# One fused layer with a local attention and a gated MLP: reordered QKV calls, another queue for three writes, and 22 identity transposes at the start

## The chip, the cores and the metric

The kernel runs on one core of one Trainium2 chip. The metric is the device time of one execution in microseconds (us). Its matrix engine is TensorE (PE in the profile, its weight loads PEld), beside VectorE (DVE), ScalarE (ACT), GpSimd (POOL) and SyncE (SP), which here only issues DMAs.

## The reference

The input x is 2048 tokens of D = 576, all in fp32. There are 32 heads of 18 columns, and the attention is local and dilated: token s looks at the 8 tokens s, s-2, ..., s-14.

```python
x = A_x
h = x + _A_ref(_layernorm(x, axis=-1), A_wqkv, A_wo)      # qkv, softmax over 8 places, times wo
h2 = h + _B_ref(_layernorm(h, axis=-1), B_w_gate, B_w_up, B_w_down)
...
g = jnp.einsum("bsd,df->bsf", x, w_gate)                  # F = 4608
u = jnp.einsum("bsd,df->bsf", x, w_up)
h = _sigmoid(g) * u
return jnp.einsum("bsf,fd->bsd", h, w_down)
```

## The kernel before

**Blocks and groups.** Even and odd tokens are apart (e = 0, 1), and each of these halves is cut in two: `BLOCKS` numbers the four blocks b = 0 to 3 of 512 tokens, (0,0), (0,1), (1,0), (1,1). A block is 4 token tiles of 128. The QKV weights are cut into four groups g of 8 heads, 432 columns each (q, k and v). A QKV *call* (b,g) is `qkv(b, g, T, w)`, lines 392 to 411: for each token tile 14 matmul passes (`tok_major`, lines 152 to 160; the fp32 operands are split into a high part `th` and a low part `tl`, so that a product takes the passes high-high, low-high and high-low), ScalarE copies the sum to `ev` (L403), and after the fourth tile the q, k and v of the call are written to DRAM scratch by three DMAs (L407, L409).

**Attention** is done by VectorE from that scratch (lines 166 to 230): SP loads q, a window of k and one of v (L176 to L178), and VectorE multiplies, reduces and normalises (L189 to L226). A generator `ag` gives it out in steps that the code takes between the QKV tiles. Its order is fixed in `att_all`: (0,0), (0,1), (1,0), (0,2), (0,3), (1,1), (1,2), (1,3), and then, under the MLP, blocks 2 and 3. The attention of (b,g) is only given out when the call (b,g) has been written (`emitted`). After (0,3) block 0 is complete, and L428 copies the tail of its rows.

**The opening** (lines 469 to 565) normalises the first tokens by chained instructions: statistics (L484 to L487, the power on POOL), `tok` (L491), transposes by the identity matrix on PE (L497, L499), the split of the transposes into `th` by ScalarE (`x_hi`, L504 and L505) and `tl` by VectorE (`x_lo`, L509 and L511), and of the first weights into high and low parts `qw` (L516, L519) from `wr`. The weights of group 1 come behind: three loads `ws` by SP (L386), split at L104 (ScalarE) and L105 (VectorE).

**The front** (L655 on) is the output projection of block 0: transposes of the attention's rows in two steps per token tile (`tr_main` L146, `tr_rest` L150), splits (L104, L105, L108, L109), the passes with `wo` and `wow`, the residual (L262), the second LayerNorm (L123 to L128) and its transposes. It is a generator `fr`, and its steps stand between the tiles of the calls (2,3) and (3,3). At its end ScalarE issues `hacc` (`h<-h`, L625) and the transposed rows (`x<-tok`, L627) to DRAM.

**The MLP** runs in units c = 0, 1, ...; its first matmuls are L746 and L753 with the weights `wf` (units 0 and 1) and `w` (unit 2 on, loaded by SP at L702 as `wg`, split at L104 and L105). The sigmoid is ScalarE's L793, the product VectorE's L766, the way down L864. Under it go, as background steps (`bg_step`, of which `skip` leaves some out), the rest of the attention and the projection of blocks 1 to 3, whose rows come back from DRAM as `oj` (L707).

**What orders the work.** The code's order, with priorities (`tc.high_priority`) and explicit "issue after" edges, goes to a scheduler, which gives each engine one list that is worked off in order; a waiting instruction holds all behind it. Releases of buffers and DMA landings are awaited in the lists.

Of the kernel before, what the change touches and what calls it, by code (L numbers as in the profile page):

```python
# [21 lines left out]
P = 128  # L22
# [9 lines left out]
TB = P * NS  # L32
# [28 lines left out]
def kernel(ctx, tc, x, wqkv, wo, wmlp, out):  # L61
    nc = tc.nc
    dve, act, pool, pe, sp = nc.vector, nc.scalar, nc.gpsimd, nc.tensor, nc.sync
# [14 lines left out]
    ident = cst.tile([P, P], F32, name="ident")  # L78
# [12 lines left out]
    qscr = [[dr.tile([P, NS * CG], F32, name=f"q{b}_{g}") for g in range(NG)] for b in range(4)]  # L91
# [61 lines left out]
    def tok_major(ps, n, th, tl, js, wh, wl):  # L153
        k = 0
        for c in range(4):
            for a, m in ((th, wh), (tl, wh), (th, wl)):
                pe.matmul(ps[:, :n], a[:, c, js], m[:, c], start=k == 0, stop=False)  # L157
                k += 1
        pe.matmul(ps[:, :n], th[:, 4, js], wh[:, 4], start=False, stop=False)
        return pe.matmul(ps[:, :n], th[:, 4, js], wl[:, 4], start=False, stop=True)  # L160
# [71 lines left out]
    def step(gen, n):  # L232
        for _ in range(n):
            if next(gen, END) is END:
                return
# [58 lines left out]
    def th_tile():  # L294
        return xt.tile([P, 5, TB], F32R, tag="th", bufs=3, name="th")

    def tl_tile():
        return xt.tile([P, 4, TB], F32R, tag="tl", bufs=4, name="tl")
# [24 lines left out]
    def mm_tile():  # L323
        return psp.tile([P, 512], F32, tag="mm", bufs=3, name="mm")

    def acc_tile():
        return psp.tile([P, 512], F32, tag="acc", bufs=5, name="acc")
# [7 lines left out]
    def ev_tile(shape):  # L335
        return sar.tile(shape, F32, tag="ev", bufs=2, name="ev")
# [59 lines left out]
    def qkv(b, g, T, w):  # L396
        e, hf = BLOCKS[b]
        ev = ev_tile([P, 3, NS, CG])
        for j in range(NS):
            ps = acc_tile()  # L400
            passes.append(tok_major(ps, NQ, *T, slice(j * P, (j + 1) * P), w[:, 0], w[:, 1]))
            with tc.high_priority(HI):
                act.activation(ev[:, :, j], ps[:, :NQ].rearrange("p (t c) -> p t c", t=3), AF.Copy)  # L403
            yield
        r0 = LP + hf * TB
        with tc.high_priority(HI):
            act.dma_start(qscr[b][g], ev[:, 0].rearrange("p j c -> p (j c)"))  # L407
            for t, s in ((1, kscr), (2, vscr)):
                act.dma_start(s[e][g][r0:r0 + TB, :].rearrange("(p j) c -> p (j c)", p=P),  # L409
                              ev[:, t].rearrange("p j c -> p (j c)"))  # L410
        emitted.add((b, g))

# [27 lines left out]
    ag = att_all()  # L440
    T = []
# [11 lines left out]
    def heads(order, ws, n):  # L453
        for b, g in order:
            for _ in qkv(b, g, T[b], ws[g]):
                step(ag, n)

    def opening():
        xb = load_x(0, (0, 1))
        wr = raw_w(0)  # L460
        load_x(0, (2, 3), xb)
        th, tl = th_tile(), tl_tile()
        xn = tok_tile()
        qw = saw.tile([P, 2, 5, NQ], F32R, tag="qw", bufs=2, name="qw")
        T.append((th, tl))
        w.append(qw)
        last = {}

        def ch(key, fn):
            with ExitStack() as way:  # L470
                way.enter_context(tc.high_priority(3 * HI))
                if key in last:
                    way.enter_context(tc.issue_after(getattr(last[key], "ins", last[key])))
                last[key] = fn()

        nr, pv, pr = {}, {}, {}

        def stats(j):
            bs = sm.tile([P, 2, 6], F32, bufs=4, name="bs")
            mv = sm.tile([P, 2], F32, bufs=4, name="mv")  # L480
            rstd = sm.tile([P, 1], F32, bufs=4, name="rstd")
            nr[j] = mv[:, 0:1], rstd
            for k in range(2):
                ch(dve, lambda: dve.bn_stats(bs[:, k], xb[:, j, k * DH2:(k + 1) * DH2]))  # L484
            ch(dve, lambda: dve.bn_aggr(mv, bs))
            ch(dve, lambda: dve.tensor_scalar(rstd, mv[:, 1:2], EPS, None, ALU.add))
            ch(pool, lambda: pool.tensor_tensor(rstd, rstd, mhalf, ALU.pow))  # L487

        def norm(j):
            m, r = nr[j]  # L490
            ch(dve, lambda: dve.tensor_scalar(xn[:, j, :D], xb[:, j], m, r, ALU.subtract, ALU.mult))  # L491
            ch(dve, lambda: dve.tensor_copy(xn[:, j, D:DX], xn[:, j, DM:D]))

        def tr(j):
            pv[j], pr[j] = mm_tile(), acc_tile()
            for c in range(4):
                ch(pe, lambda: pe.transpose(pv[j][:, c * P:(c + 1) * P],  # L497
                                            xn[:, j, c * P:(c + 1) * P], ident))
            ch(pe, lambda: pe.transpose(pr[j][:, :P], xn[:, j, DM:DX], ident))  # L499

        def x_hi(j):
            js = slice(j * P, (j + 1) * P)
            pv[j] = pv[j].rearrange("p (c n) -> p c n", c=4)
            ch(act, lambda: act.activation(th[:, 0:4, js], pv[j], AF.Copy))  # L504
            ch(act, lambda: act.activation(th[:, 4, js], pr[j][:, :P], AF.Copy))  # L505

        def x_lo(j):
            js = slice(j * P, (j + 1) * P)
            ch(dve, lambda: dve.tensor_tensor(tl[:, :, js], pv[j], f32(th[:, 0:4, js]),  # L509
                                              ALU.subtract))  # L510
            ch(dve, lambda: dve.tensor_tensor(th[64:128, 4, js], pr[j][64:128, :P],  # L511
                                              f32(th[64:128, 4, js]), ALU.subtract))
            ends.append(last[dve])

        def w_hi(c):
            ch(act, lambda: act.activation(qw[:, 0, c], wr[:, c], AF.Copy))  # L516

        def w_lo(c):
            ch(dve, lambda: dve.tensor_tensor(qw[:, 1, c], wr[:, c], f32(qw[:, 0, c]),  # L519
                                              ALU.subtract))  # L520

        call = qkv(0, 0, T[0], qw)
        ends = []

        def heads_of(j):
            ch(pe, lambda: (next(call), passes[-1])[1])

        stats(0)
        stats(1)
        norm(0)  # L530
        w_hi(0)
        tr(0)
        norm(1)
        w_hi(1)
        tr(1)
        w_lo(0)
        w_hi(2)
        w_lo(1)
        x_hi(0)
        x_lo(0)  # L540
        w_hi(3)
        w_lo(2)
        w_hi(4)
        stats(2)
        x_hi(1)
        w_lo(3)
        w_lo(4)
        heads_of(0)
        with tc.high_priority(3 * HI):
            n3, r3, sq = ln_stats(xb[:, 3], xn[:, 3])  # L550
        norm(2)
        tr(2)
        x_lo(1)
        heads_of(1)
        x_hi(2)
        ch(act, lambda: act.activation(xn[:, 3, :D], xb[:, 3], AF.Identity, bias=n3, scale=r3))
        ch(act, lambda: act.activation(xn[:, 3, D:DX], xn[:, 3, DM:D], AF.Copy))
        x_lo(2)
        tr(3)
        heads_of(2)  # L560
        x_hi(3)
        x_lo(3)
        heads_of(3)
        drain(call)
        return ends

    w = []
# [15 lines left out]
    w.append(qkv_w(2, wr))  # L583
    wr = raw_w(3)
    pads(2)
    heads(((2, 1), (3, 1)), w, 2)
    w.append(qkv_w(3, wr))
    pads(3)
    h = load_x(0)
    wos = [None, wo_w(1, swo.tile([P, 2, 5, DH2], F32R, tag="wo", name="wo1"))]  # L590
    heads(((0, 2), (0, 3), (1, 2), (2, 2), (3, 2)), w, 2)
    wos[0] = wo_w(0, saw.tile([P, 2, 5, DH2], F32R, tag="qw", bufs=2, name="wow"))

    banks = [0]
# [46 lines left out]
    fr = front()  # L641
# [10 lines left out]
        step(ag, 1)  # L652
    last = passes[-1]
    with tc.issue_after(getattr(last, "ins", last)):
        for _ in range(2):  # L655
            next(fr)
    for b in (2, 3):
        for j, _ in enumerate(more if b == 2 else qkv(b, 3, T[b], w[3])):
            with ExitStack() as way:
                if (b, j) == (2, 0):  # L660
                    way.enter_context(tc.issue_after(getattr(passes[-1], "ins", passes[-1])))
                next(fr, END)
            step(ag, 1)
        if b == 2:
            with tc.high_priority(2 * HI):
                wg = xt.tile([P, WC], F32, tag="tl", bufs=4, name="wg0")
                sp.dma_start(wg, wmlp[0])
                ww = first_split(wg)
# [377 lines left out]
    c = 0  # L1046
# [201 lines left out]
    for c, (kind, p, f) in enumerate(items):  # L1248
        w, d = wc
        for b, late_c in ((0, NF + NSTD - 3), (1, NF + NSTD + 5)):  # L1250
            if c == late_c:
                e, hf = BLOCKS[b]
                paced(ov[e, hf], hacc[b])
        skip = ((2, 3) if c == 0 else ()) if kind == "std" else (3,)
        by_seven = c >= NF + NSTD
        if c == NSTD:
            finish_bg()
# [110 lines left out]
```

## Time and profile before

| | us |
|---|---|
| three runs: median (lowest to highest) | 1578.9 (1578.4 to 1580.97) |
| the profiled execution, its own time | 1584.01 |
| its span on the core | 1582.2 |
| outside the span (1584.01 - 1582.2) | 1.8 |
| PE busy | 1551.0 (98%) |
| DVE busy | 1255.2 (79%) |
| ACT busy | 879.2 (56%) |
| POOL busy | 199.9 (13%) |

Every row of the timeline reads: start in us, length in us, engine, line, operation, output<-inputs, shape, xcount, and in brackets the time that the engine was idle before it and whose work it waited for. An engine with a q behind its name (SPq, ACTq) is issuing a DMA. A row with x4 or x5 is a run of such instructions.

### The profile page before, as it was taken

How to read it: one execution, taken by the hardware profiler on the slowest of the kernel's cores; microseconds unless marked ns; L12 is line 12 of the kernel's file. 1: busy time of each engine (PE TensorE's matmuls, PEld its weight loads, DVE VectorE, ACT ScalarE, POOL GpSimd, SP SyncE). 2: the span in 40 equal slices, each digit the busy share in tenths (PEclk: the TensorE clock that was granted, in tenths of full speed). 3: DMA queues.
4: the chain of work that ended last, by engine and by line, in shares of the span. 5: the costliest groups of instructions: out<-in, count | busy, mean ns of one | idle time of the engine just before them, and what ended most of it. 6: DMA issues, size and time to landing. Idle time of an engine off the chain costs nothing.

```text
span 1582.2 us, 22347 instructions
## 1 busy us (share of the span) xinstructions
PE 1551.0 (98%) x8520; PEld 1377.3 (87%) x8520; DVE 1255.2 (79%) x1883; ACT 879.2 (56%) x1584; POOL 199.9 (13%) x249
## 2 busy tenths in 40 slices
PE   8999999999999999999999999999999999999998
PEld 7999888887888888888888888888888888888887
DVE  6998999969999999999426588866777776677755
ACT  6632244435555645566542355766777766777660
POOL 2300000020000010000101010112112112111210
PEclk9999999999999999999999999999999999999999
DMA  8646445365566677664683524999899989999983
GB/s 284 215 168 220 179 185 190 108 235 183 133 167 170 164 176 192 157 162 109 161 242 125 181 81 126 193 181 177 170 180 186 173 173 181 173 173 186 181 169 120
DMA packets 77147, 273.95 MB, mean 173 GB/s; under 512 B 8336, under 2 KB 14224, under 8 KB 76144
## 3 DMA queue, kind: packets, MB, share of 16 engines
q0 software_dynamic: 28192, 107.29, 37.5%
q1 hardware_dynamic: 41216, 145.11, 27.2%
q10 hardware_dynamic: 7632, 20.12, 3.3%
q8 instruction: 66, 1.08, 0.3%
q14 instruction: 41, 0.34, 0.1%
HBM read 143.98 MB, written 130.87 MB: 174 GB/s over the span
## 4 chain that ended last, share of the span: by engine, by line
PE 58%; issue 16%; DVE 11%; DMA 8%; POOL 4%; ACT 2%; SPq 0%; ACTq 0%; POOLq 0%; DVEq 0%
PE b L746 27%; PE dp L864 13%; PE dp L926 6%; PE b L753 5%; PE acc L157 4%; POOL h L935 3%; DMA wg<-in_wmlp_dram 3%; DVE pr L189 2%; DVE pr L215 1%; DVE lg L193 1%; DVE w L105 1%; DVE pr L221 1%; PE b L157 1%; PE bgp L157 1%; DMA x<-tok 1%
## 5 line engine op out<-in xcount | busy, mean ns | idle before, releaser
L746 PE MATMUL b<-tl,w 128*128 128x512 f32 x1704 | 432.6, 393 | 5.1 <-ACT s L820 3.2
L746 PEld LDWEIGHTS b<-tl,w 128*128 128x128 f32 x1704 | 307.9, 188 | 63.6 <-ACT s L820 4.7
L746 PE MATMUL b<-th,w 128*128 128x512 f32 x1344 | 346.2, 392 | 1.5 <-DVE s L839 1.5
L746 PEld LDWEIGHTS b<-th,w 128*128 128x128 f32 x1344 | 244.8, 188 | 46.5 <-DVE s L839 1.9
L932 ACT ACTIVATE ev<-dp 128x576 f32<-128x576 f32 x224 | 144.7, 646 | 63.2 <-PE dp L926 58.9
L753 PE MATMUL b<-th,w 128*128 128x512 f32 x568 | 175.7, 390 | 0.0
L104 ACT ACTIVATE w<-wg 128x384 fp32r<-128x384 f32 (+1 forms) x186 | 110.8, 601 | 111.1 <-PE b L753 48.8
L935 POOL DMA_DIRECT2D h<-ev x128 | 110.0, 860 | 458.6 <-ACT ev L932 444.7
L157 PE MATMUL acc<-qw,th 128*128 128x432 f32 x512 | 154.3, 362 | 2.5 <-DVE th L109 2.3
L105 DVE TENSOR_TENSOR w<-wg,w 128x640 fp32r<-128x640 f32 (+1 forms) x186 | 120.8, 656 | 41.3 <-ACT w L104 41.1
L105 DVE TENSOR_TENSOR w<-tw,w 128x512 fp32r<-128x512 f32 x120 | 82.6, 688 | 82.1 <-ACT w L104 81.5
L753 PEld LDWEIGHTS b<-th,w 128*128 128x128 f32 x568 | 106.5, 188 | 23.2
L864 PE MATMUL dp<-d,h1h 128*128 128x288 f32 x640 | 119.9, 297 | 0.0
L864 PE MATMUL dp<-d,h0h 128*128 128x288 f32 x608 | 114.1, 297 | 0.8 <-DVE tail L874 0.8
L872 ACT ACTIVATE stage<-dp 128x576 f32<-128x576 f32 x104 | 66.9, 645 | 70.1 <-PE dp L864 69.8
L157 PEld LDWEIGHTS acc<-qw,th 128*128 128x128 f32 x512 | 96.6, 189 | 8.4 <-DVE th L109 3.5
L864 PEld LDWEIGHTS dp<-d,h1h 128*128 128x128 f32 x640 | 99.7, 190 | 3.0
L104 ACT ACTIVATE w<-tw 128x512 fp32r<-128x512 f32 x120 | 75.4, 628 | 46.5 <-PE b L746 40.0
L864 PEld LDWEIGHTS dp<-d,h0h 128*128 128x128 f32 x608 | 95.1, 190 | 4.3 <-DVE tail L874 1.0
L157 PE MATMUL acc<-qw,tl 128*128 128x432 f32 x256 | 92.6, 362 | 0.1
L189 DVE TENSOR_TENSOR pr<-kw,q 128x2304 f32<-128x2304 f32 x32 | 81.8, 2556 | 8.8 <-DMA kw<-k 8.7
L880 POOL DMA_DIRECT2D h<-stage x26 | 31.0, 1194 | 436.3 <-ACT stage L872 350.1
(310 smaller groups left out, 2955.5 us busy)
## 6 DMA issues: line engine op xcount, KB each, us to landing
h<-ev POOLq DMA_DIRECT2D x96, 576.0 KB, 7.1
wg<-in_wmlp_dram SPq DMA_DIRECT2D x47, 928.0 KB, 5.9
h<-stage POOLq DMA_DIRECT2D x26, 1152.0 KB, 9.5
wg<-in_wmlp_dram SPq DMA_DIRECT2D x36, 640.0 KB, 4.3
kw<-k SPq DMA_DIRECT2D x16, 792.0 KB, 5.2
vw<-v SPq DMA_DIRECT2D x16, 792.0 KB, 4.3
wd<-in_wmlp_dram SPq DMA_DIRECT2D x18, 576.0 KB, 7.4
h<-ev POOLq DMA_DIRECT2D x32, 288.0 KB, 6.9
```

What stands on the lines that cost most here:

```text
L104: act.activation(hi, src, AF.Copy)
L105: splits.append(dve.tensor_tensor(lo, src, f32(hi), ALU.subtract))
L157: pe.matmul(ps[:, :n], a[:, c, js], m[:, c], start=k == 0, stop=False)
L189: dve.tensor_tensor(pr, both(kw, u), q[:, us].unsqueeze(2).broadcast_to([P, 2, W, CG]), ALU.mult)
L746: pe.matmul(ps, wt[:, a, k0 + c], xx[:, m + c], start=first and k == 0, stop=k == 5, skip_group_check=True)
L753: pe.matmul(ps, wt[:, a, k0], xx[:, 4], start=False, stop=a == 1, skip_group_check=True)
L864: pe.matmul(ps[:, i, :DH2], a[:, js], d[:, m, i * DH2:(i + 1) * DH2], start=k == 0, stop=k == n)
L872: act.activation(hv, ps, AF.Copy)
L880: pool.dma_start(hacc[b], hs, accum_op=ALU.add, max_dma_last_dim=8 * D)
L926: pe.matmul(ps[:, i, :DH2], a[x][:, js], m[y], start=k in (0, 1, 3) and q == 0, stop=q == 2, skip_group_check=True)
L932: act.activation(hs[:, k % 2], ps[:, :, :DH2], AF.Copy)
L935: pool.dma_start(hsev[:, u, k0:k + 1], hs[:, :k + 1 - k0], accum_op=ALU.add, max_dma_last_dim=8 * D)
```

## The change

- The order of the QKV calls after (3,0): before (2,1), (3,1), (0,2), (0,3), (1,2), (2,2), (3,2); now (2,1), **(0,2)**, **(3,1)**, three tiles of (1,2), (0,3), the last tile of (1,2), (2,2), (3,2). The split of group 3's weights (`qkv_w(3, wr)`) still stands behind (3,1).
- The three writes of call (3,3) are issued by SP, not by ScalarE.
- In the front, one step (`tr_main` of token tile 0) is taken behind the second tile of (2,3), and the second step comes behind the next QKV tile; before, both came together.
- The MLP's unit c = 0 leaves out one background step less.
- Before all other PE work, 22 transposes of the identity into a PSUM tile that nobody reads.

```diff
         r0 = LP + hf * TB
         with tc.high_priority(HI):
-            act.dma_start(qscr[b][g], ev[:, 0].rearrange("p j c -> p (j c)"))
+            q = sp if (b, g) == (3, 3) else act
+            q.dma_start(qscr[b][g], ev[:, 0].rearrange("p j c -> p (j c)"))
             for t, s in ((1, kscr), (2, vscr)):
-                act.dma_start(s[e][g][r0:r0 + TB, :].rearrange("(p j) c -> p (j c)", p=P),
+                q.dma_start(s[e][g][r0:r0 + TB, :].rearrange("(p j) c -> p (j c)", p=P),
                               ev[:, t].rearrange("p j c -> p (j c)"))
...
         nr, pv, pr = {}, {}, {}
+        pre = mm_tile()
+        for _ in range(22):
+            ch(pe, lambda: pe.transpose(pre[:, :P], ident, ident))
...
-    heads(((2, 1), (3, 1)), w, 2)
+    heads(((2, 1), (0, 2), (3, 1)), w, 2)
     w.append(qkv_w(3, wr))
     pads(3)
     h = load_x(0)
     wos = [None, wo_w(1, swo.tile([P, 2, 5, DH2], F32R, tag="wo", name="wo1"))]
-    heads(((0, 2), (0, 3), (1, 2), (2, 2), (3, 2)), w, 2)
+    first = qkv(1, 2, T[1], w[2])
+    for _ in range(3):
+        next(first)
+        step(ag, 2)
+    heads(((0, 3),), w, 2)
+    for _ in first:
+        step(ag, 2)
+    heads(((2, 2), (3, 2)), w, 2)
...
     with tc.issue_after(getattr(last, "ins", last)):
-        for _ in range(2):
-            next(fr)
+        next(fr)
     for b in (2, 3):
         for j, _ in enumerate(more if b == 2 else qkv(b, 3, T[b], w[3])):
             with ExitStack() as way:
                 if (b, j) == (2, 0):
                     way.enter_context(tc.issue_after(getattr(passes[-1], "ins", passes[-1])))
+                    next(fr)
                 next(fr, END)
...
-        skip = ((2, 3) if c == 0 else ()) if kind == "std" else (3,)
+        skip = ((3,) if c == 0 else ()) if kind == "std" else (3,)
```

**ScalarE's list at the opening**, before:

```order
L516 ACT_TABLE_LOAD
L516 ACTIVATE qw<-wr 128x432 x3
L504 ACTIVATE th<-mm 128x4x128
L505 ACTIVATE th<-acc 128x128
L516 ACTIVATE qw<-wr 128x432 x2
L504 ACTIVATE th<-mm 128x4x128
L505 ACTIVATE th<-acc 128x128
L104 ACTIVATE qw<-ws 128x432 x2
```

and now (the lines of the changed file, so L520 is L516, L508 is L504 and L509 is L505):

```order
L520 ACT_TABLE_LOAD
L520 ACTIVATE qw<-wr 128x432 x3
L104 ACTIVATE qw<-ws 128x432 x3
L508 ACTIVATE th<-mm 128x4x128
L509 ACTIVATE th<-acc 128x128
L520 ACTIVATE qw<-wr 128x432 x2
L508 ACTIVATE th<-mm 128x4x128
L509 ACTIVATE th<-acc 128x128
```

All three splits of group 1's weights (`qw<-ws`) have moved ahead of the first `th`.

**VectorE's list at the front**, from the last attention instruction of (0,3) (`tok<-kw`) to the first splits of the projection's transposes (`tl<-mm`), before:

```order
L226 TENSOR_TENSOR tok<-kw 128x4x144
L189 TENSOR_TENSOR pr<-kw,q 128x2304
L428 COPY tok<-tok 128x64 x4
L193 TENSOR_REDUCE lg<-pr 128x128
L105 TENSOR_TENSOR tl<-mm,th 128x4x128
L109 TENSOR_TENSOR th<-acc,th 64x128 x3
```

and now:

```order
L226 TENSOR_TENSOR tok<-kw 128x4x144
L189 TENSOR_TENSOR pr<-kw,q 128x2304
L105 TENSOR_TENSOR wow<-ws,wow 128x288
L429 COPY tok<-tok 128x64 x4
L193 TENSOR_REDUCE lg<-pr 128x128
L189 TENSOR_TENSOR pr<-kw,q 128x2304
L193 TENSOR_REDUCE lg<-pr 128x128
L201 TENSOR_REDUCE mx<-lg 128x32
L105 TENSOR_TENSOR tl<-mm,th 128x4x128 x2
```

The second product and its reduction (L189, L193) and the maximum (L201) of the next attention now stand ahead of the first split.

**SP's list ahead of the MLP's first weight loads** (`wg` at the end; `vw` is the v window of an attention, `wg_2024` and `wg_2046` the weights of unit 0, `q_3_106`, `k_3_82`, `v_3_90` scratch in DRAM), before:

```order
L667 DMA wg_2024<-in_wmlp_dram 128x1856
L176 DMA q<-q_2_97 128x576
L178 DMA vw<-v_2_85 128x1584
L702 DMA wg<-in_wmlp_dram 128x1856 x3
```

and now:

```order
L678 DMA wg_2046<-in_wmlp_dram 128x1856
L178 DMA vw<-v_2_85 128x1584
L408 DMA q_3_106<-ev 128x576
L410 DMA k_3_82<-ev 128x576
L410 DMA v_3_90<-ev 128x576
L713 DMA wg<-in_wmlp_dram 128x1856 x3
```

The three writes of call (3,3) (`<-ev`) have come in ahead of the weight loads, and the q load went ahead of `wg_2046`.

## Prediction

> **What bounds the kernel now.** I read the page first, then PE's waits, then the windows, and the timeline only at the places of the change.
>
> ```profile
> span 1582.2 us, 22347 instructions
> PE 1551.0 (98%) x8520; PEld 1377.3 (87%) x8520; DVE 1255.2 (79%) x1883; ACT 879.2 (56%) x1584; POOL 199.9 (13%) x249
> ```
>
> PE is the bound: 1582.2 - 1551.0 = 31.2 us of idle time is all that any reordering can win. PE's waits say where it lies:
>
> ```profile
> PE mm L497 <- DVE tok L491: 6.6, 1, 6.6
> PE b L146 <- DMA oj<-o: 4.2, 1, 4.2
> PE acc L157 <- DVE th L109: 2.3, 2, 1.6
> PE mm L150 <- DVE tok L428: 1.7, 1, 1.7
> PE mm L150 <- DVE tok L128: 0.4, 1, 0.4
> ```
>
> The 6.6 us are the kernel's start (first loads and statistics). The change touches the start, the front (L428, L109 and L128: 1.7 + 1.6 + 0.4) and, further off, the read-back `oj`. The windows (length, PE's busy time and count, then PEld, DVE, ACT, POOL, the granted clock, DMA share, GB/s) say what the QKV stage between them is like:
>
> ```profile
> 60.00:80.00 20.00, 19.34 (x105) 17.92 (x104) 19.48 (x18) 7.76 (x19) 4.08 (x3) 1.00 0.70 237
> ...
> 120.00:140.00 20.00, 20.00 (x104) 19.15 (x103) 14.91 (x11) 3.72 (x7) 0.94 (x1) 1.00 0.72 256
> ...
> 300.00:320.00 20.00, 15.77 (x82) 13.50 (x81) 13.52 (x20) 6.75 (x12) 1.45 (x2) 0.94 0.39 136
> 320.00:340.00 20.00, 20.00 (x127) 18.57 (x126) 12.52 (x27) 6.27 (x13) 0.56 (x1) 0.89 0.67 254
> ```
>
> From 60 to 80 PE idles 0.66 us, from 120 to 140 not at all, though VectorE idles 5.1 there. Two windows at the read-back show what an idle PE costs beside the wait: a clock of 0.94 and 0.89.
>
> **The opening: +3.7 us.** The 22 transposes themselves lie in PE's first 6.6 idle us. But ScalarE's list has changed with them: the three splits of group 1 (`qw<-ws`) stand ahead of the first `th`. Before:
>
> ```profile
> 4.98 1.41 SPq L386 DMA_DIRECT2D ws<-in_wqkv_dram  x3
> 6.59 1.12 PE L497 MATMUL mm<-ident,tok 128*128 128x128 f32 x4 [6.59 <-DVE tok L491]
> 7.75 0.60 ACT L504 ACTIVATE th<-mm 128x512 fp32r<-128x512 f32 x1 [0.50 <-PE mm L497]
> 8.74 0.69 DVE L509 TENSOR_TENSOR tl<-mm,th 128x512 fp32r<-128x512 f32 x1
> 9.94 1.15 ACT L104 ACTIVATE qw<-ws 128x432 fp32r<-128x432 f32 x2
> 13.17 0.66 PE L497 MATMUL mm<-ident,tok 128*128 128x128 f32 x4
> 13.38 0.69 DVE L509 TENSOR_TENSOR tl<-mm,th 128x512 fp32r<-128x512 f32 x1
> 14.12 0.47 PE L157 MATMUL acc<-qw,tl 128*128 128x432 f32 x1
> ...
> ws<-in_wqkv_dram SPq DMA_DIRECT2D x3, 216.0 KB, 5.0
> ```
>
> The last row is of the DMA view: an issue of `ws` lands after 5.0 us (median of the three). SP's list is the same up to there, so the three land at about 9.9, 10.5 and 11.1 (issues at 4.98 to 6.0 or so, 5 us each). ScalarE now waits for them, does three splits of about 0.55 (two took 1.15 at 9.94), the last of them from 11.1, and is through at about 11.65; the first `th` starts there, not at 7.75: 3.9 us later. VectorE's first `tl` needs it and goes from 8.74 to about 12.3 (11.65 + 0.60): +3.6. From that `tl` to the second one (8.74 to 13.38, 4.64 us) VectorE's chain has next to no gap, its list has the same order there, and `tl` at 13.38 lets PE start its unbroken work at 14.12. So that start moves to about 17.7: **+3.7**. Bounds: 3.3, if the splits of `qw` by VectorE find some of their inputs earlier, and 4.4, if the loads land 0.7 late. Nothing behind covers this, since PE has 0.66 us of idle time in 60 to 80 and none later.
>
> What can the transposes win? Four transposes take 1.12 us at 6.59 and 0.66 at 13.17, so PE starts slow. Twenty-two at 1.12 / 4 = 0.28 are 6.2 us, which a start at 1.5 (when the identity is made) puts at an end of 7.7 if all are slow, and about 6.5 if the later half runs fast: no loss beside 11.65. A faster PE between 6.6 and 13 would have won nothing even in the old order, as VectorE's chain set 14.12. The Trainium skill ("TensorE: Matmul & The Clock Gate", "Part 1: The HAM clock gate") speaks for the transposes: about 3.4 us of sustained work opens the gate. By that alone, if PE were the bound of the opening, the gain would be an estimated 1 to 2 us and the sum +2 to +3 instead. The same section has the gate shut again after an idle window of that length, and the trace bears this part out: after the 4.23 us of idle time at 319.42 (below), four transposes take 1.11 us again. Between the first tiles' transposes (over by about 8) and 12.3 PE now idles some 4 us. I take 0.
>
> **The QKV order: 0.** VectorE's one large gap in the QKV stage is
>
> ```profile
> 122.93 0.76 DVE L226 TENSOR_TENSOR kw<-kw 128x576 f32<-128x576 f32 x1
> 128.47 2.56 DVE L189 TENSOR_TENSOR pr<-kw,q 128x2304 f32<-128x2304 f32 x1 [4.78 <-DMA kw<-k]
> ```
>
> where attention (0,2) waits for its k. With (0,2) ahead of (3,1) that wait goes. But PE is full there, and the number of passes is the same. VectorE comes out of the stage 4.78 earlier against +3.7 at the start: about 1.1 us earlier than before, while PE is 3.7 later. Bounds: -0.66 (the only idle time of PE there) to +0.7 (a like wait of PE).
>
> **The front: -0.2 us.**
>
> ```profile
> 178.10 0.76 DVE L226 TENSOR_TENSOR tok<-kw 128x576 f32<-128x576 f32 x1
> 184.23 0.69 DVE L105 TENSOR_TENSOR tl<-mm,th 128x512 fp32r<-128x512 f32 x1
> 187.70 2.55 DVE L189 TENSOR_TENSOR pr<-kw,q 128x2304 f32<-128x2304 f32 x1
> 188.14 0.29 PE L157 MATMUL mm<-wo,th 128*128 128x288 f32 x1
> 192.84 2.54 DVE L193 TENSOR_REDUCE lg<-pr 128x128 f32<-128x2304 f32 x1
> 196.14 0.66 DVE L201 TENSOR_REDUCE mx<-lg 128x32 f32<-128x256 f32 x1
> 199.53 2.56 DVE L215 TENSOR_TENSOR pr<-vw,lg 128x2304 f32<-128x2304 f32 x1
> 220.49 1.56 PE L746 MATMUL b<-tl,wf 128*128 128x512 f32 x6
> ```
>
> Before, the rows of block 0 were ready at 178.86, PE waited 1.7 us for their copies (L428) and 1.6 for the splits (L109): these two waits go, because VectorE is 1.1 us earlier, PE 3.7 later and a QKV tile lies between. What is late next is VectorE's list. Between `tok` and the first `tl` it now has two products and two reductions (4 x 2.55 = 10.2), the maximum (0.66), the copies and a split (0.9 in all): about 11.7 us. From 177.7 that is 189.4, `tl` ends at 190.1, and PE, which is at the projection's first passes at 188.2, waits some 1.9. Another 0.4 goes at the splits behind. Then the attention's L215 (2.56) stands ahead of the second LayerNorm of token tile 0, on which PE's transposes hang: about 1.0 + 0.2 + 0.2 in place of 0.4. Sum: -1.7 - 1.6 - 0.4 + 1.9 + 0.4 + 1.4 = 0.0, and with 0.2 of small waits that go, **-0.2**. Bounds: -3.4 (all old waits go and VectorE keeps up) to +1.5 (L215 whole ahead of the transposes). Unit c = 0 then starts at about 220.49 + 3.7 - 0.2 = 224.0.
>
> **The MLP's start: +0.3 us.** The writes of (3,3) on SP wait for ScalarE's last copy, and SP's list has the weights of unit 2 behind them.
>
> ```profile
> 217.29 0.86 SPq L702 DMA_DIRECT2D wg<-in_wmlp_dram  x2
> 220.69 0.53 ACT L403 ACTIVATE ev<-acc 128x432 f32<-128x432 f32 x1 [0.51 <-PE acc L160]
> 225.94 0.74 ACT L104 ACTIVATE w<-wg 128x640 fp32r<-128x640 f32 x1 [0.42 <-DVE df L105]
> 231.16 0.69 ACT L104 ACTIVATE d<-wg 128x576 fp32r<-128x576 f32 x1 [1.94 <-DMA x<-tok]
> 233.23 1.52 PE L746 MATMUL b<-tl,w 128*128 128x512 f32 x6
> ...
> wg<-in_wmlp_dram SPq DMA_DIRECT2D x1, 928.0 KB, 7.4
> x<-tok ACTq DMA_DIRECT2D x1, 1280.0 KB, 11.2
> ```
>
> Those loads go out at 217.29 before; now they follow the last copy (220.69 + 0.53 before, so about 224.6) and three issues, at about 226: 8.7 later. The first lands after 7.4, at 233.4, and is split (0.74, and VectorE's 0.8) by about 235.0; PE needs it at 233.23 + 3.5 = 236.7. So 1.7 us of cover is left. The writes no longer stand in ScalarE's list between the splits of `wf` and `df`, which frees ScalarE of three issues just there. I take +0.3 for the crowding of DMAs. Bounds: 0, and +4 if the loads take the 11.2 us that `x<-tok` took beside them (226 + 11.2 + 1.6 = 238.8, 2.1 late) and ScalarE's wait of 1.94 for that write grows by as much.
>
> **The step less left out: 0.** It brings attention forward in c = 0; from (1,3)'s softmax on, the two lists of VectorE and PE have the same order again. The wait at the read-back then stays:
>
> ```profile
> 227.15 0.69 DVE L766 TENSOR_TENSOR s<-s,b 128x512 f32<-128x512 f32 x1 [1.25 <-PE b L753]
> ...
> 307.78 0.75 DVE L226 TENSOR_TENSOR kw<-kw 128x576 f32<-128x576 f32 x1
> 319.42 1.11 PE L146 MATMUL b<-ident,oj 128*128 128x128 f32 x4 [4.23 <-DMA oj<-o]
> ```
>
> VectorE already waits 1.25 us for PE's gate sums in c = 0 (227.15); with PE 3.5 later that wait only grows, and the lead is spent in it.
>
> **Sum:** 3.7 + 0 - 0.2 + 0.3 + 0 = **+3.8 us**. The terms are of one execution of 1584.01 us (span 1582.2 and 1.8 outside it), 5.1 above the median of the runs. 1584.0 + 3.8 = 1587.8 by its clock; against the median, 1578.9 + 3.8 = **1582.7**.
>
> **The rivals.** (1) *The weights come late*: the loads behind the three writes land after PE needs them, and `w` of unit 2 keeps it waiting. Price: the upper bound, +4 instead of +0.3, so 1578.9 + 3.7 - 0.2 + 4 = 1586.4. For it: 1.7 us of cover only, against a spread of 7.4 to 11.2 us between landings of similar size. Against it: one wait of 1.94 was all that crowding cost before. (2) *The change does not do what the lists say it does*: ScalarE's splits find their `ws` when they are due, or VectorE's chain closes up, and PE starts dense at about 14 as before. Then the opening is 0 and the whole about 1579.0. For it: the chain of VectorE has splits that could be done in the wait. Against it: the landing near 9.9 is where ScalarE took the first one (9.94). (3) *The other side*: VectorE's lead survives. The wait of 4.78 us is gone, and the added step lets attention (1,3) end at least 4.2 us sooner relative to PE, so that `o` is written and read back before PE asks. Then 4.23 at 319.42 go, and the clock's dip with them: 0.06 x 15.8 + 0.11 x 20 is 3.1 us, of which I count 2.5, as part of that first window is idle in any case. 3.7 - 0.2 + 0.3 - 4.2 - 2.5 = -2.9: 1576.0. It decides at a VectorE lead, relative to PE, of 4.2 us at 307.78. For it: relative to PE it leads by 4.8 at the front. Against it: the front's own list gives it away, and VectorE waits for PE's gate in c = 0.
>
> **How the numbers follow.** The forecast has 0.46 (1580.3 to 1585.0), rival 1 0.17 (1585 to 1588), rival 2 0.15 (1577.5 to 1580.5), rival 3 0.22 (1572.5 to 1578.5). About 0.2%, 3.2 us, is what a measurement of this kernel can tell from no change, so the borders are 1575.7 and 1582.1. Faster: over half of rival 3, 0.12. Same: the other 0.10 of rival 3, rival 2 and 0.15 of the forecast, which lies only 0.6 above the border: 0.40. Slower: the other 0.31 of the forecast and rival 1, 0.48. The range takes in all but the ends of rivals 1 and 3: 1574.0 to 1587.5. The likeliest case alone is 1580.3 to 1585.0.
>
> **What would show it.** Right: ScalarE idle from about 7.2 to 9.9 ahead of `qw<-ws`, the first `th` at 11.6, PE dense from 17.7; no wait of 4.78 at (0,2); L146 and L157 waiting for VectorE's splits near 189; `b L146 <- oj` again above 3 us. Wrong: PE dense at 14 (rival 2), a wait for `w` or `wg` near 237 (rival 1), or no wait for `oj` near 320 (rival 3).

## The result, and the profile after

The changed kernel took 1591.8 us (median of 6 runs, 1587.3 to 1593.1) against 1580.7 for the kernel before in the same series (6 runs): 1.0063 times as long, 95% interval 1.005 to 1.0076. A second series of 12 runs (e9 below) gave 1587.4 against 1582.1: 1.0032, 1.0015 to 1.0049. So the change is slower, by 5 to 11 us; forecast was slower by 3.8 with a range that ended at 1587.5. The profiled execution took 1591.68 us, 7.7 more than that of before (1584.01).

Two lines of the page:

```profile
span 1589.8 us, 22386 instructions
PE 1558.9 (98%) x8542; PEld 1384.9 (87%) x8542; DVE 1255.8 (79%) x1883; ACT 879.1 (55%) x1584; POOL 201.5 (13%) x249
```

PE's waits (in all, how often, the longest):

```profile
PE acc L157 <- ACT th L508: 4.5, 1, 4.5
PE mm L157 <- DVE tl L105: 4.3, 1, 4.3
PE b L146 <- DMA oj<-o: 2.7, 1, 2.7
PE dp L875 <- ACT h0h L104: 2.3, 1, 2.3
PE acc L157 <- DVE qw L105: 1.0, 1, 1.0
```

PE is busy 7.9 us longer and idle as long as before (30.9 against 31.2). Of the 7.9, the 22 transposes are 4.95; they lie in the idle time at the start, where 6.6 us of waiting became 1.5, and the wait of 4.5 for `th` took its place. The other 3 us of busy time are the same matmul passes taking longer at a slower clock. Windows of 20 us, the granted clock third from the end:

```profile
0.00:20.00 20.00, 13.56 (x59) 11.84 (x60) 11.50 (x30) 10.31 (x21) 4.43 (x16) 0.83 0.72 237
180.00:200.00 20.00, 15.66 (x90) 14.94 (x89) 18.71 (x25) 5.96 (x15) 0.00 (x0) 0.91 0.71 262
280.00:300.00 20.00, 17.69 (x86) 15.04 (x85) 16.95 (x22) 8.47 (x14) 0.00 (x0) 0.91 0.28 96
320.00:340.00 20.00, 17.28 (x95) 14.73 (x94) 11.31 (x22) 8.33 (x18) 0.51 (x1) 0.91 0.88 321
```

A clock of 0.91 over 20 us is some 3.4 us at half speed ((1 - 0.91) x 20 x 2 = 3.6, rounded), 0.83 is 6.8. Such a stretch, in which the granted clock is 0.5, is called a half-clock stretch below. Each begins in or just behind one of the waits listed above. Where PE is then full, 3.4 us at half clock cost 1.7.

Where the time went, place by place. **The opening:**

```profile
1.50 4.95 PE L480 MATMUL mm<-ident 128*128 128x128 f32 x22 [1.50 <-POOL ident masks.py:199]
10.68 1.75 ACT L104 ACTIVATE qw<-ws 128x432 fp32r<-128x432 f32 x3 [3.35 <-DMA ws<-in_wqkv_dram]
12.34 0.58 ACT L508 ACTIVATE th<-mm 128x512 fp32r<-128x512 f32 x1
12.97 0.73 PE L157 MATMUL acc<-qw,th 128*128 128x432 f32 x1 [4.45 <-ACT th L508]
17.58 0.69 DVE L513 TENSOR_TENSOR tl<-mm,th 128x512 fp32r<-128x512 f32 x1
18.64 0.35 PE L157 MATMUL acc<-qw,tl 128*128 128x432 f32 x1
```

ScalarE waits 3.35 us for group 1's weights and does the first `th` at 12.34, not at 7.75; the pass that began PE's unbroken work at 14.12 begins at 18.64: +4.5. Of these, 4.2 are VectorE's second `tl`, which starts at 17.58 instead of 13.38. The other 0.3 are PE's own: it is full from 12.97 on, but the granted clock is 0.5 from 10.3 to 17.1, and it comes to that pass 0.4 after the `tl` is done (18.27). **The QKV stage:**

```profile
133.50 0.66 PE L157 MATMUL acc<-qw,th 128*128 128x432 f32 x2 [1.02 <-DVE qw L105]
145.36 1.49 ACTq L410 DMA_DIRECT2D k<-ev  x1
148.87 0.32 SPq L177 DMA_DIRECT2D kw<-k  x1
156.82 2.56 DVE L189 TENSOR_TENSOR pr<-kw,q 128x2304 f32<-128x2304 f32 x1 [4.37 <-DMA kw<-k]
```

The wait of attention (0,2) is gone, and attention (0,3) waits 4.37 us instead: its k is written at 145.36, loaded from 148.87 on, and there at 156.8. PE waits 1.02 us for group 3's split, since (0,2), which used to stand between that split and (0,3), is ahead now. **The front:**

```profile
181.57 0.76 DVE L226 TENSOR_TENSOR tok<-kw 128x576 f32<-128x576 f32 x1
193.89 1.29 DVE L105 TENSOR_TENSOR tl<-mm,th 128x512 fp32r<-128x512 f32 x2
194.64 0.61 PE L157 MATMUL mm<-wo,th 128*128 128x288 f32 x1 [4.34 <-DVE tl L105]
227.92 1.56 PE L757 MATMUL b<-tl,wf 128*128 128x512 f32 x6
```

From the end of `tok` (182.33) to the first `tl` (193.89) VectorE needs 11.6 us, as its list said (11.7), but `tok` is 3.5 us later than before, not 1.1 earlier. PE waits 4.34 and then runs at half clock. The MLP starts at 227.92, 7.4 later. **The MLP's start:**

```profile
230.36 2.54 SPq L713 DMA_DIRECT2D wg<-in_wmlp_dram  x2
239.84 0.74 ACT L104 ACTIVATE w<-wg 128x640 fp32r<-128x640 f32 x1 [1.56 <-DMA wg<-in_wmlp_dram]
281.83 2.55 DVE L189 TENSOR_TENSOR pr<-kw,q 128x2304 f32<-128x2304 f32 x1
284.30 0.68 DVE L777 TENSOR_TENSOR s<-s,b 128x512 f32<-128x512 f32 x1
285.70 0.54 PE L875 MATMUL dp<-d,h0h 128*128 128x288 f32 x2 [2.31 <-ACT h0h L104]
```

The weights go out at 230.36, 2.4 behind the MLP's start (before: 3.2 ahead of it), and are split from 239.84. The wait for them is ScalarE's, 1.56 us. Later VectorE's list has an attention product (281.83) ahead of the product of gate and up (284.30), and the way down waits 2.31 us for it, through ScalarE's split `h0h`; in e5 below, which has the three writes back on ScalarE, this wait is absent. The read-back wait is 2.72, not 4.23, and half the half-clock stretch behind it is gone. At the end the profiled execution is 7.7 us late.

### The profile page after: what moved, and what is told of

Read it like the earlier page. It is cut to its first block, busy times and chain, and to the rows that moved or that the text cites. A ratio compares the mean times of both kernels' runs of the same rounds, so it can differ in the third digit from the quotient of the medians.

```text
span 1589.8 us, 22386 instructions
## 1 busy us (share of the span) xinstructions
PE 1558.9 (98%) x8542; PEld 1384.9 (87%) x8542; DVE 1255.8 (79%) x1883; ACT 879.1 (55%) x1584; POOL 201.5 (13%) x249
## 4 chain that ended last, share of the span: by engine, by line
PE 31%; issue 30%; POOL 7%; DVE 3%; DMA 3%; ACT 1%; POOLq 0%; SPq 0%; DVEq 0%; ACTq 0%
PE b L757 15%; PE dp L875 11%; POOL h L946 7%; PE b L764 3%; DMA wg<-in_wmlp_dram 2%; PE b L157 1%; PE bgp L157 1%; DVE w L105 1%; PE dp L937 0%; DMA h<-ev 0%; DMA tail<-h 0%; DVE s L777 0%; DVE pr L215 0%; DVE lg L193 0%; DMA o<-kw 0%
## 5 line engine op out<-in xcount | busy, mean ns | idle before, releaser
L189 DVE TENSOR_TENSOR pr<-kw,q 128x2304 f32<-128x2304 f32 x32 | 81.7, 2553 | 8.7 <-DMA kw<-k 8.6
```

Source lines behind the costliest of these rows:

```text
L189: dve.tensor_tensor(pr, both(kw, u), q[:, us].unsqueeze(2).broadcast_to([P, 2, W, CG]), ALU.mult)
```

## The experiments

All are timed in series that share the runs of before. The kernel before had medians of 1581.7 to 1582.7 in these.

| run | edit | median us (runs) | ratio to before, 95% |
|---|---|---|---|
| e1 | before + 22 transposes | 1584.3 (12) | 1.0024, 1.0006 to 1.0041 |
| e2 | e1, group 1's splits held | 1581.9 (12) | 1.0004, 0.9992 to 1.0016 |
| e3 | before + order of calls | 1585.0 (12) | 1.0026, 1.0013 to 1.0038 |
| e4 | before + skip | 1574.7 (12) | 0.9959, 0.9947 to 0.9971 |
| e5 | changed, writes on ScalarE | 1587.3 (9) | 1.0039, 1.0024 to 1.0055 |
| e6 | changed, old order of calls | 1588.1 (8) | 1.0041, 1.0025 to 1.0058 |
| e7 | changed, old front | 1587.4 (12) | 1.0038, 1.0025 to 1.0051 |
| e8 | changed, old skip | 1586.2 (12) | 1.0032, 1.0015 to 1.005 |
| e9 | changed, again | 1587.4 (12) | 1.0032, 1.0015 to 1.0049 |
| e10 | before + writes on SP | 1584.8 (12) | 1.0017, 1.0001 to 1.0032 |
| e11 | before + front | 1586.3 (12) | 1.0026, 1.001 to 1.0043 |
| e12 | before + skip + front | 1584.5 (12) | 1.0016, 1.0 to 1.0032 |
| e13 | changed, group 1's splits held | 1585.7 (12) | 1.0028, 1.0011 to 1.0046 |
| e14 | changed, (0,3) ahead of (1,2) | 1594.3 (6) | 1.0084, 1.0061 to 1.0107 |
| e15 | e4 again | 1576.5 (12) | 0.9965, 0.9949 to 0.9982 |
| e16 | e2 + skip | 1578.7 (12) | 0.9976, 0.9961 to 0.9991 |

### The opening: e1, e2, e13

e1 adds the loop of 22 transposes of the diff to the kernel before, and nothing else. As built, ScalarE's three splits move ahead of the first `th`, as in the changed kernel, and the order of early loads in SP's list changes. 

> The kernel before with only the 22 identity transposes added. As built, ScalarE's three splits of group 1's weights stand ahead of the first th split, as in the changed kernel. Theory A (the transposes cost only through that order, which the scheduler changed): ScalarE waits for the weights until about 10.7, the first th comes at about 12.3, PE's unbroken work starts at about 18.6 instead of 14.4, and nothing later changes: +4.2 to +4.7 us, about 1585. Rival B (a PE that starts fast wins back part of it): the start moves by only 2 to 3 us, +2 to +3. Rival C (the transposes themselves are free and the opening is not the cause of the changed kernel's time): within 1 us of before.

One row of PE's waits:

```profile
PE acc L157 <- ACT th L507: 3.9, 1, 3.9
```

As theory A has it, PE waits 3.9 us for the first `th`. The pass that began the unbroken work stands at 19.23 in its profile, 5.1 us late: 3.8 by VectorE's second `tl` (17.19, done at 17.88), and 1.3 because PE, at half clock until 18.8, comes to the pass later than that. In the QKV stage PE is 3.8 us late; the median is 2.6 longer. e2 holds the splits (`...` stands for lines left out):

```diff
-                if after is not None:
-                    way.enter_context(tc.issue_after(getattr(after, "ins", after)))
+                for a in after or ():
+                    way.enter_context(tc.issue_after(getattr(a, "ins", a)))
...
         x_hi(1)
+        held = last[act]
...
-    done = opening()
-    w.append(qkv_w(1, None, done[1]))
+    done, held = opening()
+    w.append(qkv_w(1, None, (done[1], held)))
```

> The kernel before with the 22 transposes, and the splits of group 1's weights held behind the second x_hi by an issue-after edge, so that ScalarE's list is that of before. Theory A (order, not transposes): ScalarE does the first th at about 7.8 again, PE's unbroken work starts at about 14.1 to 14.4, total within 1 us of before. Rival B (a PE that is fast from the first tile on is worth something): 1 to 2 us faster than before. Rival D (the transposes themselves delay the start, by their length or by the clock they leave behind): about +4 as with the transposes alone.

ScalarE's first `th` and PE's first pass of the unbroken work in e2:

```profile
7.41 0.60 ACT L507 ACTIVATE th<-mm 128x512 fp32r<-128x512 f32 x1
...
14.25 0.47 PE L157 MATMUL acc<-qw,tl 128*128 128x432 f32 x1
```

and a wait of PE's further on:

```profile
PE acc L157 <- ACT ev L403: 1.7, 2, 1.4
```

The first `th` is back at 7.41 and the pass at 14.25, where it was at 14.12 without the transposes. So what the transposes cost (2.6 us in e1's median) they cost through ScalarE's list, and a PE that is fast from the first tile on wins nothing there: VectorE's chain sets that point. The time equals that of before. What is left is a wait of 1.4 near 54. It may come from this wait of ScalarE's, for loads of `ws` that SP now issues after three loads of group 2's weights; no run tests that:

```profile
21.09 0.56 ACT L104 ACTIVATE qw<-ws 128x432 fp32r<-128x432 f32 x1 [2.78 <-DMA ws<-in_wqkv_dram]
```

e13 makes the same edit in the changed kernel, where it moves the three splits in ScalarE's list and nothing else. 

> The changed kernel with the splits of group 1's weights held behind the second x_hi; only these places of ScalarE's list differ. Theory A (the opening costs the changed kernel 4 us through that order): PE's unbroken work starts near 14 instead of 18.6, the first MLP matmul comes 4 us earlier, and the time is 3 to 5 us shorter than the changed kernel: about 1584, 1 to 3 above before. Rival (VectorE and the loads behind it keep the later places anyway): the 4 us are given back before or at the MLP's start, within 1 us of the changed kernel.

```profile
PE mm L157 <- DVE tl L105: 3.3, 1, 3.3
...
PE acc L157 <- ACT ev L403: 1.5, 1, 1.5
```

The pass is back at 14.23, but PE meets the 1.5 us near 55, and the MLP starts at 225.6: 2.3 earlier than in the first profile of the changed kernel, 1.0 earlier than in its second (e9, 226.57). Against the runs of before in its own series the median is 3.0 longer, where e9's is 5.3 longer. By the medians the opening costs the changed kernel 2.3 us, below the 3 to 5 of theory A; but the intervals overlap, and neither theory A nor its rival (within 1 us of the changed kernel) is excluded.

### The order of the calls: e3, e6, e14

e3 takes the two hunks on `heads` and `first` alone. 

> The kernel before with only the new order of the QKV calls. Theory A (the wait moves from attention (0,2) to (0,3)): the 4.78 us wait for k at attention (0,2) is gone, one of about 4.4 stands at (0,3), PE waits about 1.0 for the split of group 3's last weights at the first tile of (0,3), and at the front PE waits about 4 us for VectorE's first tl split (two products, two reductions and a maximum ahead of it) and then runs some 3.4 us at half clock, in place of the old 3.7: +1.3 and +1.4, together +2.5 to +4. Rival (the step of the prediction): no wait takes its place, VectorE comes out of the stage about 4.8 us earlier, PE's waits at the front shrink: -1 to 0 us.

PE and VectorE in e3:

```profile
128.67 0.66 PE L157 MATMUL acc<-qw,th 128*128 128x432 f32 x2 [1.02 <-DVE qw L105]
...
150.48 2.56 DVE L189 TENSOR_TENSOR pr<-kw,q 128x2304 f32<-128x2304 f32 x1 [2.86 <-DMA kw<-k]
...
187.27 0.48 PE L150 MATMUL acc<-ident,tok 128*128 128x128 f32 x1 [4.45 <-DVE th L109]
```

All three waits of theory A are there; the one at (0,3) is 2.86, not 4.4. VectorE does come out of the stage earlier, but by 2.9 us (`tok` at 175.24 instead of 178.10) and not by 4.78; its list at the front has the second product ahead of the splits, and PE waits 4.45. The front's first two steps still come together in e3, with no QKV tile between them to fill that wait, and 6.8 us at half clock begin in it. The median is 3.2 us longer, in the range of theory A. So the step of the prediction that lets the wait at (0,2) go without another in its place does not hold.

e6 undoes the same hunks in the changed kernel. 

> The changed kernel with the old order of the QKV calls, all else as changed. Theory A: VectorE's wait for k is back at attention (0,2) and gone at (0,3); PE's wait of 1.0 for group 3's split goes; at the front only one product and one reduction stand ahead of the first tl split, so PE's wait of 4.3 for it falls to about 1 or less and the half-clock stretch with it: 3 to 5 us faster than the changed kernel, about 1587. Rival (the order of the calls does not matter while PE is full): within 1 us of it.

```profile
PE b L750 <- DVE s L770: 7.4, 2, 5.8
...
PE acc L150 <- DVE tl L105: 2.1, 1, 2.1
```

and two waits of other engines:

```profile
132.31 2.56 DVE L189 TENSOR_TENSOR pr<-kw,q 128x2304 f32<-128x2304 f32 x1 [5.47 <-DMA kw<-k]
365.04 0.74 ACT L104 ACTIVATE w<-wg 128x640 fp32r<-128x640 f32 x1 [7.60 <-DMA wg<-in_wmlp_dram]
```

The wait for `qw` is gone, the wait for k is back at (0,2) at 5.47, and the wait at the front falls from 4.3 to 2.1, where 1 or less was forecast; the MLP starts at 222.8, 5.1 earlier. But PE loses 7.4 us to VectorE's `s` later (two waits, 1.5 at 234 and 5.8 at 368). Ahead of the second, ScalarE waits 7.60 for a weight load. In all no gain over e9: the time won ahead of the MLP is given back behind its start.

e14 puts the late call (0,3) first:

```diff
-    first = qkv(1, 2, T[1], w[2])
-    for _ in range(3):
-        next(first)
-        step(ag, 2)
-    heads(((0, 3),), w, 2)
-    for _ in first:
-        step(ag, 2)
-    heads(((2, 2), (3, 2)), w, 2)
+    heads(((0, 3), (1, 2), (2, 2), (3, 2)), w, 2)
```

> The changed kernel with call (0,3) ahead of the three tiles of (1,2), right behind (3,1). Theory A (VectorE's 4.4 us at attention (0,3) is the wait for that call's writes): the call ends about three tiles (8.2 us) earlier, that wait is gone, VectorE reaches the front some 4 us earlier and PE's wait for the first tl split there falls from 4.3 to about 1; but PE waits 3 us or more for group 3's splits at the first tile of (0,3), so that the whole is within 3 us of the changed kernel. Rival (the wait at (0,3) is a full queue or a slow load): it stays at 4 us.

```profile
124.25 0.47 PE L157 MATMUL acc<-qw,th 128*128 128x432 f32 x1 [2.88 <-ACT qw L104]
130.03 1.09 PE L157 MATMUL acc<-qw,th 128*128 128x432 f32 x2 [3.93 <-DVE qw L105]
...
151.84 2.56 DVE L189 TENSOR_TENSOR pr<-kw,q 128x2304 f32<-128x2304 f32 x1 [2.79 <-DMA kw<-k]
```

PE pays 6.8 us for group 3's splits, which uses up most of the 8.2 us by which the call was to come earlier: its k is written at 141.97, 3.4 before the 145.36 of the changed kernel. The wait at (0,3) shrinks from 4.37 to 2.79 and does not go. It follows the call's writes, as theory A says, but the sum (1594.3) is 7 us above e9, more than the 3 that A allowed. Weights that come late and a call that comes late are the two ends of one trade.

### The front, the queue and the skip: e10, e11, e4, e15

e10 takes the hunk with `q = sp` alone. 

> The kernel before with only the three writes of call (3,3) on SP. Theory A (they hold the first weight loads of the MLP, rival 1 of the prediction): the first wg load goes out some 5 us after the MLP's first matmul instead of 3 us before it, PE waits 2 to 3 us for wf or w in units 0 to 2, and the time is 2 to 5 us longer. Rival (the prediction's step: 1.7 us of cover holds): PE does not wait for weights, within 1 us of before.

```profile
227.17 2.17 SPq L703 DMA_DIRECT2D wg<-in_wmlp_dram  x2
...
236.24 2.93 PE L747 MATMUL b<-tl,wf 128*128 128x512 f32 x6 [3.05 <-DVE s L767]
```

The MLP starts at 223.5 there, `wg` goes out 3.7 later, VectorE stands 5.8 us waiting for the split of those weights, and PE 3.05 for VectorE. This is rival 1 of the prediction. The wait for the read-back is only 0.6 there, so part of the loss comes back; the median is 2.7 us longer, and the interval (1.0001 to 1.0032) only just leaves out no change.

e11 takes the two hunks on `next(fr)` alone. 

> The kernel before with only the tile of (2,3) between the front's two steps. Theory A: PE's 1.70 us at the transposes of the tails is filled by that tile, and its wait for the splits behind stays at 1 to 2 us, since VectorE's list decides when they are done: 1 to 2 us faster than before. Rival (the wait only moves: PE comes to the splits sooner and waits there the same 3.4 us): within 0.7 us of before.

```profile
217.69 1.55 PE L746 MATMUL b<-tl,wf 128*128 128x512 f32 x6
...
220.60 2.37 SPq L702 DMA_DIRECT2D wg<-in_wmlp_dram  x2
...
231.87 0.74 ACT L104 ACTIVATE w<-wg 128x640 fp32r<-128x640 f32 x1 [4.88 <-DMA wg<-in_wmlp_dram]
```

and one of PE's waits there:

```profile
PE b L746 <- ACT s L793: 2.6, 1, 2.6
```

The front does its part: the MLP starts at 217.69, 2.8 us earlier, more than theory A asked. But the weight load goes out at 220.60, later than before (217.29), since SP's list has a v window ahead of it that VectorE releases. ScalarE waits 4.88 for it, PE 2.6, another 2.6 follows for `h0h` near 280, and the kernel is 4.3 us slower. The forecast of the time fails; as in e6 and e10, a weight load comes late.

e4 takes the hunk on `skip` alone, and e15 is e4 once more. 

> The kernel before with only the changed skip in unit c = 0. Theory A (one attention product now stands ahead of the product of gate and up in unit c = 2, so the way down waits): a PE wait for h0h or h0l of about 2 us near 275 to 285, and the read-back wait (4.2 before) shorter by about 1.5 to 2.5 as the attention is no later while PE is: 0 to +1 us in all. Rival (the step of the prediction): no new wait, the read-back as before, within 0.5 us. Second rival: the read-back wait goes and nothing takes its place, -3 to -5 us.

> The kernel before with only the new skip, once more, on another chip. Theory A (the added step lets attention (1,3) end some 6.7 us sooner after the MLP's start, so that the read-back wait of 4.2 and the half-clock stretch behind it go): 5 to 7 us faster than before again, read-back wait below 1 us. Rival (luck of one series): within 2 us of before.

The read-back in e4, and the same wait in e15:

```profile
303.38 0.75 DVE L226 TENSOR_TENSOR kw<-kw 128x576 f32<-128x576 f32 x1
...
312.48 0.66 PE L146 MATMUL b<-ident,oj 128*128 128x128 f32 x4 [0.52 <-DMA oj<-o]
```

```profile
PE b L146 <- DMA oj<-o: 0.5, 1, 0.5
```

Attention (1,3) ends 81.3 us after the MLP's start (304.1 - 222.8), against 88.0 before (308.5 - 220.5); the wait of 4.23 becomes 0.5 and no half-clock stretch follows. The new wait that theory A saw near 280 is 1.0 at 240. In two series this edit alone is 7.1 and 6.1 us faster. Both medians lie above the 3 to 5 of the second rival and near the 6.7 that rival 3 of the prediction gave the read-back, but the intervals (4.6 to 8.4 and 2.8 to 8.1) reach into the second rival's range. The lead that the prediction saw spent in c = 0 is used there: VectorE's list has the reduction of the next attention at 227.04 (e4), where before it waited 1.25 us for PE ahead of the product `s`.

### What is left: e5, e7, e8, e9, e12, e16

e5 (`q = act`), e7 (both `next(fr)` together) and e8 (`skip` as before) undo one hunk each in the changed kernel; e9 is the changed kernel unaltered.

> The changed kernel with the three writes of call (3,3) back on ScalarE. Theory A (the writes on SP hold the first weight loads, and with them the whole chain of weight splits behind the matmuls): the first wg load goes out near 224 instead of 230.4, the first w split of ScalarE at about 234 instead of 239.8, the wait for h0h at 285.7 (2.3) shrinks below 0.5, attention (1,3) ends some 4 to 6 us earlier relative to the MLP's start, and the read-back wait (2.7) all but goes: 4 to 7 us faster than the changed kernel, about 1586. Rival (the queue makes no difference: there is 1.7 us of cover, as the prediction had it): within 1 us of the changed kernel, about 1591.

> The changed kernel with the front's first two steps together again, as before the change. Theory A (the tile between them only fills a wait that VectorE's list makes): PE waits about 2.7 us more at its transposes or splits and 2.7 less behind them, the front as long as in the changed kernel within 1 us: about 1591. Rival (the tile between the steps costs or saves a wait of its own): 2 us or more to either side.

> The changed kernel with the old skip in unit c = 0. The skip alone made the kernel before 6.5 us faster. Theory A (in the changed kernel that gain is eaten by late weights, which hold VectorE in the attention of (1,3)): giving it up costs only 0 to 3 us, and the read-back wait is back at 3 us or more: 1591 to 1595. Rival (the skip's gain is there in the changed kernel as well, and the other parts cost 15 us together): about 6 us slower than the changed kernel, 1598.

> The changed kernel unaltered, to see how far its time moves from one series of runs to the next. The kernel with the old skip in it, whose lists differ from it by one swap of two neighbours on VectorE, had a median of 1586.2. Theory A (the six first runs lay high, by chance of which idle times brought a half-clock stretch): a median of 1586 to 1590. Rival (the skip does cost the changed kernel some 5 us): 1591 or more.

e5: the wait for `h0h` near 285 is gone, yet 2.7 us for `s` near 370, 1.6 for `h0l` near 245 and 3.2 at the read-back stand in the list instead. Within 1 us of e9, so theory A's 4 to 7 us are not there. e7: PE waits 5.47 at the splits in place of 4.34, and the MLP starts at 228.5, 0.6 from the changed kernel, as theory A said. e8:

```profile
PE dp L875 <- ACT h0h L104: 3.0, 1, 3.0
PE b L146 <- DMA oj<-o: 2.7, 1, 2.7
```

These are much the same waits as in the changed kernel. Its lists differ from that kernel's by one swap of neighbours on VectorE, near 316: in the changed kernel the skip hardly moves anything, so that e8 is, but for that swap, a third series of the same kernel, and its 1586.2 with e9's 1587.4 says that the first 1591.8 lay high. Theory A of e9 holds. All three undone hunks leave the time where e9 has it.

e12 and e16 look for a faster version. 

> The kernel before with the new skip and the tile between the front's two steps, without the transposes, the new order and the SP writes. If the gains of the skip alone (6.5 us) and of the front (up to 2) add up: about 1573 to 1575, faster than both kernels. Rival (the lists behind the front are rearranged by every edit, so that gains do not add): anywhere between 1574 and 1584, with a read-back wait of 2 us or more back.

> The kernel before with the new skip and the held transposes. Theory A (the transposes are worth nothing when the order is held): as the skip alone, within 1 us. Rival (a faster PE in the opening adds to it): 1 to 2 us faster than the skip alone.

e12 brings the read-back wait back at 2.8 and adds 5.2 us of waits for VectorE's `s`: the gains do not add. Its 1584.5 lies just past the range of its rival (1574 to 1584). e16 is 2.2 us slower than e15 and has a wait of 1.5 us near 54, as e2 has; but the intervals overlap, and e2 is no slower than before, so a cost of the held transposes is not shown. The fastest version is e4 alone, 0.4% below before and about 0.7% below the changed kernel.

## Why the prediction was wrong

It had the sign and the largest term, and missed the size by a factor of 2.9 in the first series (1.4 in the second).

- **Opening, +3.7: right, too small.** 4.5 measured, just beyond the upper bound of 4.4. The loads of `ws` were there at 10.68, 0.8 later than taken, and the first `th` came at 12.34, 0.7 later. PE at half clock added 0.3 (1.3 in e1): the prediction saw PE idle for some 4 us there and took 0 for it. e1 and e2 show that the order in ScalarE's list costs it, not the transposes.
- **"VectorE comes out of the stage about 1.1 us earlier": this is the step that failed.** The wait of 4.78 did not go; it moved from (0,2) to (0,3), at 4.37. I asked what hides the wait that goes and not when the call that now comes last is written. e3, the order of calls by itself, shows the same, with 2.86 us at (0,3). The wait of 1.02 for `qw` is beyond the bound of 0.7 too. PE comes to the front's transposes at 185.42, not 179.39: 6.0 us late, of which 4.5 are the opening, 1.0 the wait for `qw` and 0.4 a wait for ScalarE's `ev` at 57.
- **The front, -0.2: wrong through that step.** VectorE's 11.7 us between `tok` and `tl` were right (11.6). But `tok` ended at 182.33, 4.6 later than taken (177.7). PE, itself 2.1 later than taken at the projection's first passes (190.3, not 188.2), waited 4.34, not 1.9. A stretch of 3.4 us at half clock came with that wait, which I had charged to the read-back only. Of the 7.4 us at the MLP's start, 6.0 come from ahead of the front and 1.4 from the front: its waits are 0.6 longer (4.34 against 1.70 + 1.65 + 0.39), the half clock costs some 1.7, and about 0.9 is won back at places that I have not found.
- **The MLP's start, +0.3: mechanism right (rival 1), place wrong.** The loads left at 230.36 instead of 226. PE did not wait for the weights but for VectorE, 45 us behind their first split, for 2.3 us; e10 prices the writes at 2.7 by themselves.
- **The skip, 0: right for the changed kernel** (e8), though not because VectorE's lead is spent: the lists are nearly the same either way. In the kernel before it is worth 6 to 7 us, which I had given rival 3 a chance of 0.22 for.
- **The read-back stays: half right.** It shrank by 1.5, and the half-clock stretch with it from 6.8 to 3.4 us. That gave back some 3 us (1.5 and 1.7) of the 10.2 by which the kernel was late ahead of it.
- **31.2 us of idle time as "all that any reordering can win": not so.** Time at half clock counts as busy. e4, whose wait was 4.23 us, is 6 to 7 us faster, and its PE is busy 1549.5 us in place of 1551.0.

How large the miss was depends on the series. Forecast was +3.8; the first series has +11, the later ones of the same lists, but for one swap in e8, +5.3 (e9) and +4.5 (e8). So some 6 us of the first are that this series lay high, and no step of the prediction accounts for them. The +5.3 on the base of the prediction, 1578.9, would be 1584.2, inside its range. That it comes so near is partly luck: the read-back gave back some 3 us of what the order of calls and the MLP's start had cost on top of the forecast.

What stays open is how the single costs make up the whole: from the kernel before, the five parts alone measure +2.6, +3.2, -7.1, +2.7 and +4.3 (e1, e3, e4, e10, e11), a sum of 5.7, close to the 5 of e9; yet in the changed kernel none of the four parts that were undone (the order of calls, the queue, the front, the skip) gives its share back, and no run undoes two of them, or leaves out the transposes. Each edit has the scheduler lay the lists anew, so that the sum may be near by chance.

## What to carry to other kernels

Where a stall at one step goes, date the next step's input too: here the call that was put back delivered the next attention's k late, and the wait came again 28 us on. An edit on one engine can cost through another's list: read all lists of the built kernel, and hold what has slipped ahead of a wait by an explicit order; here this alone brought the time back to that of before (e2). Time that is won ahead of a stage whose weights are loaded just in time can come back as a wait for them (e6, e11), so look at when those loads are issued. Moving them first was not tried here.

## What the hardware showed besides

Executions of one kernel differ by up to 13 us over the series, and much of that goes with the matmul clock. Over the 127 runs of before in these series (1574.3 to 1587.9), the 16 runs with a mean granted clock of 0.999 or 1.0 have a median near 1577, the 33 at 0.996 one of 1582.2, the 8 at 0.993 one of 1586.4. A stretch at half clock lasted 3.4 or 6.8 us in these profiles (10.2 once, in the opening of e9), and followed idle times of only 1.8 to 2.3 us in some (2.31 at 285.70 in the changed kernel; 1.82 near 398 in e7) while one of 2.81 brought none (e9 at 325); the changed kernel, with the same lists, has 2.72 at that place and a stretch behind it. The Trainium skill ("TensorE: Matmul & The Clock Gate", "Part 1: The HAM clock gate") has a free-running window of 3.4 us; the lengths agree with it, and a window that runs free would make a wait costly in one execution and cheap in the next. The idle times of 1.8 to 2.3 us are shorter than that window, and here the measurement decides: they can bring a stretch. The changed kernel's clock was 0.993 on the mean of its 18 runs, before 0.996, the skip alone 0.998: (1 - clock) x 1580 is 10.5, 5.7 and 2.4 us. In the profile of the changed kernel 3.4 us of its lost clock lie in the opening, in the stretch from 10.3 to 17.1; PE is idle in it to 12.97 and full behind that. The clock column does not show everything: in the kernel before, the four transposes at 6.59 take 1.12 us, against 0.66 at 13.17, with a stated clock of 1.00.
